# A two-layer spectral and MLP network on one core: weight table with the zero frequency kept in its rows, and a rewritten step order for the first layer

## The chip, the cores and the metric

The kernel runs on one core of one Trainium2 chip. A core has a matrix engine (PE, with its weight loads listed apart as PEld), three elementwise engines (DVE, ACT, POOL), a queue engine that mostly starts transfers (SP), and DMA engines that all queues share. The metric is device time in microseconds (us); lower is better. The time before is the median of six runs.

## The reference

The input `x` has 2048 rows of 512 bf16 values. Two layers are applied, each made of a spectral filter and an MLP mixer, with the same weights in both:

```python
def _A_ref(x, w_r, w_i):
    B, S, D = x.shape
    X = jnp.fft.rfft2(x.astype(jnp.float32), axes=(-2, -1))
    X = X * (w_r + 1j * w_i)
    return jnp.fft.irfft2(X, s=(S, D), axes=(-2, -1)).astype(jnp.bfloat16)

def _B_ref(x, w1, w2, w3, w4):
    h = _gelu(_layernorm(x) @ w1)          # 512 -> 512
    hs = shifted_quarters(h) @ w2          # each quarter of h moved by -1, +1, -2, +2 rows
    x1 = x + hs
    return x1 + _gelu(_layernorm(x1) @ w3) @ w4   # 512 -> 1792 -> 512

for _ in range(2):
    x = x + _A_ref(_layernorm(x), A_w_r, A_w_i)
    x = x + _B_ref(_layernorm(x), B_w1, B_w2, B_w3, B_w4)
```

The filter weights `A_w_r` and `A_w_i` are 2048 x 257: one value for each of 2048 sequence frequencies and 257 feature frequencies, of which number 0 is the constant term. The layer norm takes the mean away, so that the constant term of every row is zero and the kernel works with the 256 frequencies 1 to 256 only.

## The kernel before

**Layout.** Row s = 16p + q of `x` lies in partition p, slot q, of `x_state`. The two-dimensional transform is split into three products with small tables: over p, over d (the feature index) and over q. The frequencies are then held in 32 index pairs j, two of which make one of 16 blocks b.

**Start.** `load_all` (L152) issues all loads on SP's queue: eight pieces of `x`, table FA, half of table TL, and then the filter weights in four chunks of eight j (`for lo in range(0, NH, 8)`, L174), each chunk for the real plane (pl 0) and the imaginary one (pl 1), with two halves of table TR and the rest of TL in between; at the end come G and Tinv. `load_W` (L200) fills partitions 0 to 31 of the tile `W` from rows 64m + j (L205), and partitions 32 to 63 from rows 64m + 64 - j, in falling order (L206; the row for j = 0 apart, L208). Partitions 64 to 127 are a copy of 0 to 63, made by a transfer within SBUF that POOL issues (L209); these eight copies are put off with `K.later` until the first front has been issued. `W` is 128 x 2 x 32 x 256 bf16, and each j of a plane takes 256 neighbouring values. `load_mlp` (L185) issues on SP a tiny transfer that reads the last chunk's copy in `W`, and behind it the four MLP weight matrices.

**First front.** `first_front` (L391) does layer norm statistics and the product over p for the first layer (`over_p`, results moved to tile V). `wake` and `fill` (L219, L230) run matmuls on a tile of zeros to keep PE busy.

**A layer.** `layer` (L441) runs a hand-written list of steps, `ORDER_A` for the first layer and `ORDER_B` for the second. Each token is a letter (the step), a number (which block, unit or row), a PSUM bank after a dot, or A or V for ACT or DVE. The schedule is manual: instructions enter each engine's queue in the order of the list and every engine works through its queue in order. A unit is one block (0, 1, 14, 15) or two (2, 4, 6, 8, 10, 12). The steps of the spectral part are:

- `d` (L455): product over d of a unit on PE, L462; `t` moves it to SBUF (tile TV) on ACT or DVE.
- `q` (L476): product over q on PE, L486; `x` moves it to tile X.
- `p` (`weigh`, L493): two DVE products of X with `W`, one for each plane, into tile PB (L501). This is the step that needs the filter weights.
- `N` (`negate`): negates a half of TR on DVE (L698), needed by `b`.
- `b` (L504): back over q on PE, L510; `m` moves it to tile M.
- `D` (L523): back over d on PE, L528. It contracts over the frequencies for one slot of M, which holds part of every block, so that the first `D` waits for the last `m`.
- `Y`, `P`, `a`: move, back over p (L540), and add to `x_state` (L548).

Then come norm, transposes, and the MLP: `v` and `h` (first matrix, L579, and gelu), `u` and `f` (second matrix, L595), `w` and `g` (third, L630), `W` and `A` (fourth, L643, and the sum). During the first layer's MLP sixteen steps `L` (`permute`, L687) reorder the frequencies inside `W` for the second layer: one DVE copy out to a tile X (L692) and one back (L693). At the end of the first layer, `O` and `G` do the second layer's product over p.

Of the kernel before, what the change touches and what calls it, by code (L numbers as in the profile page):

```python
# [13 lines left out]
BF16 = dt.bfloat16  # L14
FP32 = dt.float32

P = 128
# [5 lines left out]
NH = 32  # L23
# [75 lines left out]
def kernel(  # L99
# [24 lines left out]
    K.bank, K.next_bank = None, 0  # L124
    ctx.enter_context(tc.manual_schedule())
    load_all(K, A_x, A_w_r, A_w_i, B_w1, B_w2, B_w3, B_w4)
    make_hT(K)
    wake(K)
    first_front(K)
    for last in (False, True):  # L130
# [21 lines left out]
def load_all(K, A_x, A_w_r, A_w_i, B_w1, B_w2, B_w3, B_w4):  # L152
    nc = K.nc
    tabs = dft_tables()
    dram = {k: nc.inline_tensor(v, name="tab_" + k).ap() for k, v in tabs.items()}

    def table(k, eng):
        t = K.const.tile(list(tabs[k].shape), BF16, name=k)
        eng.dma_start(t[:], dram[k])
        setattr(K, k, t)  # L160

    K.x = K.big.tile([P, NQ, D], BF16, name="x_state")
    xv = A_x[0].rearrange("(p q) d -> p q d", q=NQ)
    table("T", nc.scalar)
    for h in range(8):
        nc.sync.dma_start(K.x[:, h * 2:h * 2 + 2, :], xv[:, h * 2:h * 2 + 2, :])  # L166
    table("FA", nc.sync)
    K.TL = K.const.tile(list(tabs["TL"].shape), BF16, name="TL")
    K.TR = K.const.tile([P, 3, NH, 64], BF16, name="TR")
    load_q = lambda k, sl: nc.sync.dma_start(getattr(K, k)[:, sl], dram[k][:, sl])  # L170
    load_q("TL", slice(0, 8))
    K.W = K.const.tile([P, 2, NH, 256], BF16, name="W")
    K.later = []
    for lo in range(0, NH, 8):  # L174
        for pl, w in enumerate((A_w_r, A_w_i)):
            load_W(K, w, pl, lo, lo + 8)
        if lo == 8:
            load_q("TL", slice(8, 16))
        if lo in (0, 16):
            nc.sync.dma_start(K.TR[:, 0:2, lo:lo + 16], dram["TR"][:, :, lo:lo + 16])  # L180
    for k in ("G", "Tinv"):
        table(k, nc.sync)
    K.load_G2 = lambda: nc.sync.dma_start(K.G[:], dram["G2"])

    def load_mlp():  # L185
        gate2 = K.const.tile([1, 16], BF16, name="gate2")
        nc.sync.dma_start(gate2[:], K.W[64:65, 1, NH - 1, 0:16])
        for k, w, n, c in (("w1", B_w1, 4, D), ("w2", B_w2, 4, D), ("w3", B_w3, 4, FH), ("w4", B_w4, 14, D)):
            t = K.const.tile([P, n, c], BF16, name=k)
            nc.sync.dma_start(t[:], w.rearrange("(t p) n -> p t n", p=P))  # L190
            setattr(K, k, t)

    K.load_mlp = load_mlp
    K.eps = K.const.tile([P, 1], FP32, name="eps")
    nc.vector.memset(K.eps[:], EPS)
    K.mhalf = K.const.tile([P, 4], FP32, name="mhalf")
    nc.gpsimd.memset(K.mhalf[:], -0.5)


def load_W(K, w, pl, lo, hi):  # L200


    v = w.rearrange("(m j) f -> m j f", j=64)[:, :, 1:257]
    j1 = max(lo, 1)
    K.nc.sync.dma_start(K.W[0:32, pl, lo:hi], v[:, lo:hi])  # L205
    K.nc.sync.dma_start(K.W[32:64, pl, j1:hi], v[:, 65 - hi:65 - j1][:, ::-1])  # L206
    if lo == 0:
        K.nc.sync.dma_start(K.W[32:64, pl, 0], v[:, 32])  # L208
    K.later.append(lambda: K.nc.gpsimd.dma_start(K.W[64:128, pl, lo:hi], K.W[0:64, pl, lo:hi]))  # L209


# [7 lines left out]
def wake(K):  # L219

    nc = K.nc
    t = K.const.tile([P, 256], BF16, name="zeros")
    nc.vector.memset(t[:], 0.0)
    one = K.small.tile([P, 1], FP32, name="wake")
    nc.scalar.activation(one[:], K.eps[:], ACT.Sqrt, bias=0.0, scale=1.0)
    K.zeros = t
    fill(K, WAKE)


def fill(K, n):  # L230
    for i in range(n):
        K.nc.tensor.matmul(K.ps[:, 7 if K.bank is None else K.bank, 0:256], lhsT=K.zeros[:, 0:P], rhs=K.zeros[:], start=True, stop=True)


class Stats:
# [155 lines left out]
def first_front(K):  # L391
# [26 lines left out]
    def front(k):  # L418
        ps[k] = over_p(K, FIRST[k])
        if k in FILL:  # L420
            fill(K, FILL[k])
# [19 lines left out]
def layer(K, last):  # L441
# [3 lines left out]
    nc = K.nc  # L445
# [47 lines left out]
    def weigh(u):  # L493
        n = len(UNITS[u])
        x = X.pop(u)[:, :, 0:256 * n].rearrange("p h (n f) -> p h n f", f=256)
        pab[u] = []
        for pl in range(2):
            t = PB[:, n_pab[0] % 8]
            n_pab[0] += 1
            w = K.W[:, pl, 2 * u:2 * u + 2 * n].rearrange("p (n h) f -> p h n f", h=2)  # L500
            nc.vector.tensor_tensor(t[:, :, 0:n], x, w, op=ALU.mult)  # L501
            pab[u].append(t)

# [182 lines left out]

    def permute(k):  # L687

        w = K.W[:, k // 8, 4 * (k % 8):4 * (k % 8) + 4]
        t = K.stream.tile([P, 4, 256], BF16, name="X", bufs=2)  # L690
        tw = t[:]
        nc.vector.tensor_copy(tw.rearrange("p b (h f) -> p b h f", h=2), w.rearrange("p b (f h) -> p b h f", h=2))  # L692
        nc.vector.tensor_copy(w, tw)  # L693

    def negate(k):
# [3 lines left out]

    next_V = {}  # L700
    table = {"d": over_d, "t": take_d, "q": over_q, "x": take_q, "p": weigh, "b": back_q,
             "D": back_d, "Y": take_D, "P": back_p, "a": add_x, "s": stats2, "r": rstd2, "c": lambda g: ln[g].ratio(), "n": norm2,
             "T": tr, "v": w1, "h": gelu1, "u": w2, "f": add_x1, "k": square3, "E": resid,
             "R": rstd3, "o": norm3, "U": tr3, "w": w3, "g": gelu3,
             "m": take_b, "W": w4, "A": add_x2, "y": store, "B": stats4, "j": aggr4, "S": rstd4, "Q": scale_T,
             "O": front, "G": take_front, "L": permute, "N": negate}
    for op in (ORDER_B if last else ORDER_A).split():
        op, _, bank = op.partition(".")
        K.bank = int(bank) if bank else None
        if op[0] == "X":  # L710
            fill(K, int(op[1:]))
            continue
        if op[0] in FLEX:
            table[op[0]](int(op[1:-1]), op[-1])
        else:
            table[op[0]](int(op[1:]))
# [16 lines left out]
Q15V O3 Q14V G4A O5 G3V O7 G5A O8 G8A G7V  # L733
"""
ORDER_A = """
d4.0 d1.2 d2.4 t1A q1.2 t2A t4V x1V q4.0 d10.6 q2.4 x4A p1 t10V d6.2 d12.0 q10.6 x2A t6A p4 N0 d8.4 q6.2 t12A t8A
b1.0 x10V d15.1 p2 b4.6 b3.7 m1A x6A b5.0 m4A t15V d14.1 q8.2 m3A b2.6 p10 d0.7 m5A N1 p6 q12.4 b10.0 t14V x8A
q15.2 x12A t0A p8 m2A x15A b11.1 m11A p12 q0.4 b6.7 b8.6 m6A p15 x0A q14.2 x14V b7.1 m10A b9.7 m7A m9A b13.4 p0
b15.5 b12.0 p14 m15A m15V m12A b0.1 b14.7 m8V m13V m0A m14A D2.4 D3.6 Y3A D0.0 Y2V P4.4 a4 Y0A P7.5 P6.6 P5.7 D1.0
a7 a6 a5 D4.4 s4 P0.6 Y1V s7 P1.7 s6 a0 s5 P3.0 Y4A r1 a1 P2.1 s0 a3 P8.6 P9.7 a2 D5.4 a8 D7.0 n7V n6V n5V T3 s1  # L740
n4V s3 s2 T2 r0 a9 D6.2 Y5A P11.6 Y7A s8 P10.4 P15.5 Y6A P13.7 a11 a10 s11 n2V n3V a15 n0V P14.6 n1A a13 c1 s10
P12.4 s9 r2 a12 s15 L7 a14 v3.2 n10V s12 n9V s13 s14 T1 v2.4 h3 n8A T0 n11V L12 r3 h2 n12V v1.6 h1 v0.2 T5 h0 c0
n15V n14A u3.6 T4 u2.7 u1.2 v5.4 f1 n13V u0.3 L15 h5 v4.0 f2 T7 T6 f3 E2 f0 u4.2 E3 v6.6 h4 k1 f4 L6 L1 v7.2 k3
u5.0 E4 c3 u6.1 k0 f5 E0 u7.4 k2 c2 R0 h7 h6 E1 o0V f6 k4 o1V o2A u10.5 u9.0 f7 u8.1 o3V u14.4 u12.6 f10 k5 f8
u11.1 U0 L9 k6 k7 f9 u13.5 R1 E5 u15.0 f12 E7 f14 f13 U1 E9 E8 w4.6 o4A E6 f11 L5 o5V o6V o7A w0.4 k10 k8 k9 w5.2
g0 E13 w1.4 f15 E14 k12 U3 E11 k11 k13 U2 g4 E12 k14 w2.0 E10 w6.6 R2 g5 w7.2 g1 o9V g7 o11V g6 k15 w3.4 g2 o10A R3
g3 o8A L0 w13.2 w9.6 w12.0 L3 w11.4 o14A E15 U4 g13 g12 L10 o13V U5 g11 W1.0 g9 W2.1 W3.6 L11 o15A w10.4 w8.2 L4
g10 o12V L2 L13 A1 g8 L8 A3 A2 W0.4 w14.2 A0 B2 W5.5 B0 L14 B3 g14 U6 W7.4 A5 B1 A7 B7 w20.2 w19.4 j1 j2 W6.0 j0 j7
g19 W4.1 U7 A6 g20 w15.2 w24.4 w21.6 B5 A4 g21 g15 w16.0 B6 j3 B4 w17.6 w23.2 g16 j6 w27.0 j5 g17 g27 w18.6 j4 g18
S0 w25.0 Q0 W9.6 Q3 S1 W10.7 g25 A10 g24 Q2 B10 w22.4 W8.7 Q1 g23 A9 Q4 O1.2 g22 Q7 w26.4 Q6 B9 W11.6 O0.0 G1A j9  # L750
Q5 g26 G1V A8 B8 O2.4 G0A A11 B11 G2A j11 W14.7 W12.6 j10 G2V A14 B14 j14 j8 G0V A12 S14 Q14 B12 W15.7 j12 A15 B15
j15 W13.6 O14.7 S2 S12 Q9 Q11 O3.0 Q12 S15 Q8 Q10 O4.4 G14A G3A Q15 A13 B13 G4A j13 G3V S13 O5.6 X4.2 O15.2 Q13 G4V
G15V G5A G15A X4.3 O6.6 G6A X8.3
"""
ORDER_B = """
d15.0 t15A d4.2 q15.0 x15V d1.4 t4A d8.6 t1A q1.4 q4.2 p15 t8A x1V b15.0 d12.6 x4A p1 m15V m15A q8.4 t12A d10.0
# [45 lines left out]
```

## Time and profile before

| What | us |
|---|---|
| Median of 6 runs | 365.51 |
| Lowest and highest of them | 363.57, 367.26 |
| The profiled execution's own time | 365.26 |
| Its span, first to last instruction | 363.3 |
| PE busy in the span | 344.1 |
| ACT busy | 199.2 |
| DVE busy | 183.5 |
| First layer: first `d` product to first `D` product (L462 at 22.38, L528 at 49.36) | 26.98 |
| Second layer: the same (L462 at 199.08, L528 at 219.74) | 20.66 |
| The eight copies L209, issue to landing (least, median, greatest) | 4.0, 8.2, 8.8 |

Start times are counted from the span's start. Busy time on PE includes the matmuls on zeros. The time of a run is about 2 us longer than the span, so that a change in the span is a change in the time.

### The profile page before, as it was taken

What the parts mean: (1) busy time and instruction counts of PE and PEld (TensorE: products, weight loads), DVE (VectorE), ACT (ScalarE), POOL (GpSimd) and SP (SyncE); (2) the same over time, 40 slices, a digit from 0 to 9 for tenths busy, and PEclk for the clock granted to TensorE, in tenths of its full rate; (3) what the DMA queues carried; (4) which work ended last, traced back from release to release, by engine and by line L of the source; (5) the groups of instructions that cost most, each with busy time, mean ns of one, the idle gap of its engine ahead of it and who ended that gap; (6) DMA issues with size and microseconds to landing.
All of it is one profiled execution on the core that took longest, in us unless ns stands there. A gap on an engine that the chain in (4) does not pass through costs nothing.

```text
span 363.3 us, 5613 instructions
## 1 busy us (share of the span) xinstructions
PE 344.1 (95%) x2124; PEld 188.9 (52%) x2124; DVE 183.5 (50%) x453; ACT 199.2 (55%) x343; POOL 67.0 (18%) x171
## 2 busy tenths in 40 slices
PE   7798698899999999999998999999999999999996
PEld 5676487434444444444546788734444444444442
DVE  3866679758965342402677797846680031100122
ACT  6868669968579122054304997987785510247100
POOL 1211006752331000200031000781450000000000
PEclk9899899999999999999999999999999999999999
DMA  7999594540234200000000000452322032000012
GB/s 240 241 229 219 153 362 99 97 87 14 47 58 88 58 0 2 0 0 2 1 2 0 2 2 0 78 109 51 58 52 38 0 58 74 0 29 2 29 43 87
DMA packets 47274, 24.60 MB, mean 68 GB/s; under 512 B 34832, under 2 KB 44048, under 8 KB 47248
## 3 DMA queue, kind: packets, MB, share of 16 engines
q1 hardware_dynamic: 46464, 22.09, 26.2%
q0 software_dynamic: 640, 2.10, 2.6%
q8 instruction: 16, 0.26, 0.3%
q14 instruction: 10, 0.08, 0.1%
q10 hardware_dynamic: 144, 0.07, 0.1%
HBM read 11.67 MB, written 2.10 MB: 38 GB/s over the span
## 4 chain that ended last, share of the span: by engine, by line
PE 73%; DMA 10%; ACT 9%; DVE 3%; issue 2%; SPq 1%; POOL 0%; ACTq 0%; DVEq 0%; POOLq 0%
PE ps L630 27%; PE ps L643 26%; PE ps L595 8%; PE ps L579 5%; ACT junk L258 4%; DMA W<-in_A_w_i_dram 3%; PE ps L510 2%; DMA W<-W 2%; DMA TL<-tab_TL 2%; PE ps L462 2%; PE ps L486 2%; DMA W<-in_A_w_r_dram 2%; PE ps L528 2%; ACT Y L149 1%; SPq L166 1%
## 5 line engine op out<-in xcount | busy, mean ns | idle before, releaser
L637 ACT ACTIVATE gT<-ps 128x1024 bf16<-128x1024 f32 x56 | 54.9, 1023 | 86.5 <-PE ps L630 86.5
L643 PE MATMUL ps<-w,gT 128*128 128x512 bf16 x448 | 98.8, 379 | 0.0
L630 PE MATMUL ps<-xT,w 128*128 128x512 bf16 x448 | 98.6, 379 | 0.0
L648 DVE TENSOR_TENSOR x_state<-ps,x_state 128x512 bf16<-128x512 f32 x32 | 21.7, 689 | 121.1 <-PE ps L643 121.0
L630 PEld LDWEIGHTS <-w 128*128 128x128 bf16 x448 | 43.8, 98 | 52.6
L643 PEld LDWEIGHTS <-gT 128*128 128x128 bf16 x448 | 43.8, 98 | 52.6
L579 PE MATMUL ps<-xT,w 128*128 128x512 bf16 x128 | 29.2, 379 | 1.4 <-ACT hT L586 0.9
L603 DVE SCALAR_TENSOR_TENSOR xn<-xn,ln_c,ps 128x512 bf16<-128x512 bf16 x32 | 23.1, 744 | 13.2 <-PE ps L595 8.9
L595 PE MATMUL ps<-w,hT 128*128 128x512 bf16 x128 | 29.0, 379 | 0.8 <-ACT hT L586 0.8
L501 DVE TENSOR_TENSOR PB<-X,W 128x1024 bf16<-128x1024 bf16 (+1 forms) x40 | 21.3, 579 | 5.2 <-DMA W<-W 1.7
L258 ACT ACTIVATE junk<-x_state 128x512 bf16<-128x512 bf16 x36 | 22.6, 629 | 1.1
L548 DVE SCALAR_TENSOR_TENSOR x_state<-ps,x_state 128x512 bf16<-128x512 f32 x32 | 20.5, 686 | 3.5 <-PE ps L540 3.5
L258 ACT ACTIVATE junk<-xn 128x512 bf16<-128x512 bf16 x32 | 20.1, 627 | 3.6 <-DVE xn L603 3.1
L586 ACT ACTIVATE hT<-ps 128x512 bf16<-128x512 f32 x32 | 17.5, 607 | 7.9 <-PE ps L579 7.9
L246 DVE BATCH_NORM_STATS2 ln_st<-x_state 128x6 f32<-128x512 bf16 x28 | 18.7, 685 | 4.9 <-DMA x_state<-in_A_x_dram 4.7
L579 PEld LDWEIGHTS <-w 128*128 128x128 bf16 x128 | 12.3, 98 | 16.6 <-issue 1.5
L595 PEld LDWEIGHTS <-hT 128*128 128x128 bf16 x128 | 12.4, 98 | 16.4 <-ACT hT L586 1.2
L510 PE MATMUL ps<-TR,PB 128*128 128x128 bf16 x256 | 18.1, 225 | 3.0 <-DVE TR L698 1.8
L510 PEld LDWEIGHTS <-PB 128*128 128x128 bf16 x256 | 15.5, 101 | 6.6 <-issue 4.6
L149 ACT ACTIVATE V<-ps 128x1024 bf16<-128x1024 f32 (+2 forms) x11 | 9.5, 884 | 15.8 <-PE ps L351 14.1
L281 POOL TENSOR_SCALAR ln_ve<-ln_mv 128x4 f32<-128x4 f32 (+1 forms) x15 | 3.9, 261 | 76.9 <-DVE ln_mv L274 76.2
L462 PE MATMUL ps<-FA,V 128*128 128x256 bf16 x128 | 16.3, 273 | 1.7 <-ACT V L149 1.7
(73 smaller groups left out, 388.7 us busy)
## 6 DMA issues: line engine op xcount, KB each, us to landing
w<-in_B_w_dram SPq DMA_DIRECT2D x2, 1792.0 KB, 13.5
x_state<-in_A_x_dram SPq DMA_DIRECT2D x8, 256.0 KB, 5.6
W<-W POOLq DMA_DIRECT2D x8, 256.0 KB, 8.2
out_dram<-x_state SPq DMA_DIRECT2D x16, 128.0 KB, 1.8
TR<-tab_TR SPq DMA_DIRECT2D x2, 512.0 KB, 9.2
w<-in_B_w_dram SPq DMA_DIRECT2D x2, 512.0 KB, 4.2
W<-in_A_w_r_dram SPq DMA_DIRECT2D x7, 128.0 KB, 8.5
W<-in_A_w_i_dram SPq DMA_DIRECT2D x7, 128.0 KB, 9.5
```

The costliest lines, as they stand in the source:

```text
L258: K.nc.scalar.activation(junk[:], src, ACT.Square, bias=0.0, scale=D ** -0.5, accum_out=self.s[:, i, 1:2])
L462: nc.tensor.matmul(oi[:, 1 - h], rhs=K.FA[:, t, h], lhsT=V[:, 2 * t + h, 2 * b:2 * b + 2].rearrange("d b q c -> d (b q c)"), start=(t == 0 ...
L501: nc.vector.tensor_tensor(t[:, :, 0:n], x, w, op=ALU.mult)
L510: nc.tensor.matmul(o[:, (2 * h + F) * P:(2 * h + F + 1) * P], lhsT=pab[u][k][:, h, b - u, F * P:(F + 1) * P], rhs=K.TR[:, k:k + 2, 2 * b + ...
L548: nc.vector.scalar_tensor_tensor(K.x[:, q, :], ps.pop(("P", q)), 1.0, K.x[:, q, :], op0=ALU.mult, op1=ALU.add, accum_out=ln[g].s[:, i, 0:1])
L579: nc.tensor.matmul(o[:, i], lhsT=K.w1[:, t, j * P:(j + 1) * P], rhs=xT[g][:, :, t, :], start=(t == 0), stop=(t == 3))
L595: nc.tensor.matmul(o, lhsT=K.hT[:, j, st:st + P], rhs=K.w2[:, j, :], start=(j == 0), stop=(j == 3))
L603: nc.vector.scalar_tensor_tensor(xn[:, q, :], xn[:, q, :], ln[q // 4].c[:, q % 4:q % 4 + 1], ps.pop(("u", n)), op0=ALU.mult, op1=ALU.add, ...
L630: nc.tensor.matmul(o[:, i], lhsT=K.w3[:, c, t * P:(t + 1) * P], rhs=xT3[g][:, :, c, :], start=(c == 0), stop=(c == 3))
L637: nc.scalar.activation(gT[g][:, 2 * j:2 * j + 2, :], ps.pop(("w", k)), ACT.Gelu_apprx_tanh, bias=0.0, scale=1.0)
L643: nc.tensor.matmul(o, lhsT=gT[g][:, t, i * P:(i + 1) * P], rhs=K.w4[:, t, :], start=(t == 0), stop=(t == 13))
L648: nc.vector.tensor_tensor(K.x[:, q, :], ps.pop(("W", n)), K.x[:, q, :], op=ALU.add)
```

## The change

`W` is widened to 257 values for each j. The weights' view `v` in `load_W` keeps all 257 columns. The load of partitions 0 to 31 now takes eight whole rows of 257, which lie one behind the other both in DRAM and in the tile. The loads of partitions 32 to 63 still take columns 1 to 256 of each row, now into positions 1 to 256 of the tile's rows. Position 0 in partitions 32 to 63 is set to zero on POOL at the start, since the copy to partitions 64 to 127 reads whole rows. `weigh` and `permute` read and write positions 1 to 256, so that the rows they use begin at an odd element of the tile, 514 bytes apart.

The tile of zeros is cut from 256 to 128 columns, and `fill` reads it twice for one matmul.

`ORDER_A` is replaced by another list of the same 475 steps: other order, other banks, and another choice of ACT or DVE for 26 of the moves and norms. `ORDER_B` and `ORDER_0` are the same.

```diff
-    K.W = K.const.tile([P, 2, NH, 256], BF16, name="W")
+    K.W = K.const.tile([P, 2, NH, 257], BF16, name="W")
     K.later = []
+    nc.gpsimd.memset(K.W[32:64, :, :, 0:1], 0.0)
...
-    v = w.rearrange("(m j) f -> m j f", j=64)[:, :, 1:257]
+    v = w.rearrange("(m j) f -> m j f", j=64)
     j1 = max(lo, 1)
     K.nc.sync.dma_start(K.W[0:32, pl, lo:hi], v[:, lo:hi])
-    K.nc.sync.dma_start(K.W[32:64, pl, j1:hi], v[:, 65 - hi:65 - j1][:, ::-1])
+    K.nc.sync.dma_start(K.W[32:64, pl, j1:hi, 1:257], v[:, 65 - hi:65 - j1, 1:257][:, ::-1])
     if lo == 0:
-        K.nc.sync.dma_start(K.W[32:64, pl, 0], v[:, 32])
+        K.nc.sync.dma_start(K.W[32:64, pl, 0, 1:257], v[:, 32, 1:257])
     K.later.append(lambda: K.nc.gpsimd.dma_start(K.W[64:128, pl, lo:hi], K.W[0:64, pl, lo:hi]))
...
-    t = K.const.tile([P, 256], BF16, name="zeros")
+    t = K.const.tile([P, P], BF16, name="zeros")
...
-        K.nc.tensor.matmul(K.ps[:, 7 if K.bank is None else K.bank, 0:256], lhsT=K.zeros[:, 0:P], rhs=K.zeros[:], start=True, stop=True)
+        K.nc.tensor.matmul(K.ps[:, 7 if K.bank is None else K.bank, 0:256], lhsT=K.zeros[:], rhs=K.zeros[:].unsqueeze(1).to_broadcast([P, 2, P]), start=True, stop=True)
...
-            w = K.W[:, pl, 2 * u:2 * u + 2 * n].rearrange("p (n h) f -> p h n f", h=2)
+            w = K.W[:, pl, 2 * u:2 * u + 2 * n, 1:257].rearrange("p (n h) f -> p h n f", h=2)
...
-        w = K.W[:, k // 8, 4 * (k % 8):4 * (k % 8) + 4]
+        w = K.W[:, k // 8, 4 * (k % 8):4 * (k % 8) + 4, 1:257]
...
 ORDER_A = """
-d4.0 d1.2 d2.4 t1A q1.2 t2A t4V x1V q4.0 d10.6 q2.4 x4A p1 t10V d6.2 d12.0 q10.6 x2A t6A p4 N0 d8.4 q6.2 t12A t8A
-b1.0 x10V d15.1 p2 b4.6 b3.7 m1A x6A b5.0 m4A t15V d14.1 q8.2 m3A b2.6 p10 d0.7 m5A N1 p6 q12.4 b10.0 t14V x8A
-q15.2 x12A t0A p8 m2A x15A b11.1 m11A p12 q0.4 b6.7 b8.6 m6A p15 x0A q14.2 x14V b7.1 m10A b9.7 m7A m9A b13.4 p0
-b15.5 b12.0 p14 m15A m15V m12A b0.1 b14.7 m8V m13V m0A m14A D2.4 D3.6 Y3A D0.0 Y2V P4.4 a4 Y0A P7.5 P6.6 P5.7 D1.0
...
+d1.0 d0.1 d4.2 t1A t0V q0.0 x0V q1.4 d6.6 x1V t4A p0 d2.0 t6A q4.4 d10.2 t2V q6.6 x4A p1 N0 p4 d8.4 t10A t8V x6A p6
+q2.0 b1.2 b4.3 m1A d12.6 b0.2 m4A d14.3 x2A q10.4 t12A p2 d15.0 b5.1 t14V x10A m0V q8.6 b2.3 b6.4 x8A m2A m6A m5A
+q12.6 q14.2 N1 p10 b7.5 t15A p8 b10.4 m7V b11.1 b3.0 x12A m11A x14V p12 p14 m3A b8.5 m8A q15.6 m10A b9.2 x15A p15
+b12.3 b13.5 m12A m9A b14.4 m13V b15.3 m15V m14A m15A D0.2 D1.4 Y1A Y0V D3.6 P1.2 P0.3 P2.4 a1 P3.5 Y3A a0 a2 a3
...
```

## The prediction

> **What bounds the kernel now.** I read the page first, for where PE has gaps; then a table of busy times by stage; then the waits and the order of time of DVE in the stage that stood out.
>
> ```profile
> span 363.3 us, 5613 instructions
> PE   7798698899999999999998999999999999999996
> ```
>
> PE is full from about 80 us on, apart from a dent near 195. What can be won lies in the first eight slices of 9.1 us. Stages, from the table of windows (columns: busy us and count for PE, PEld, DVE, ACT, POOL, then clock, DMA share, GB/s):
>
> ```profile
> 22.30:30.00 7.70, 7.62 (x78) 5.82 (x79) 4.66 (x6) 5.87 (x7) 1.03 (x3) 1.00 1.09 229
> 30.00:38.00 8.00, 6.63 (x81) 4.47 (x79) 4.81 (x8) 4.87 (x7) 1.02 (x2) 1.00 0.98 197
> 38.00:49.40 11.40, 7.82 (x100) 6.40 (x101) 9.54 (x19) 8.73 (x15) 0.00 (x0) 0.85 0.68 229
> 49.40:69.20 19.80, 18.74 (x149) 14.37 (x150) 16.33 (x46) 17.42 (x40) 9.25 (x27) 1.00 0.63 169
> 94.80:189.60 94.80, 94.80 (x458) 43.71 (x457) 43.16 (x106) 37.48 (x52) 11.07 (x22) 1.00 0.10 20
> 199.10:219.80 20.70, 19.84 (x257) 15.36 (x258) 16.89 (x30) 18.45 (x27) 0.00 (x0) 1.00 0.01 2
> ```
>
> The first three rows are the first layer's stage from the first `d` to the first `D`: 27.1 us, PE busy 22.1. The last row is the same stage of the second layer, with the weights long in place: 20.7 us. So at most 27.0 - 20.7 = 6.3 us are to be had there; the MLP row (94.8 of 94.8) has nothing to give. DVE in the first of these stages, waits and then single products:
>
> ```profile
> DVE PB L501 <- DMA W<-W: 1.7, 1, 1.7
> DVE X L147 <- PE ps L486: 1.7, 2, 1.3
> DVE TV L147 <- PE ps L462: 1.5, 1, 1.5
> DVE PB L501 <- DMA W<-in_A_w_r_dram: 1.4, 1, 1.4
> ...
> 28.57 0.69 DVE L501 TENSOR_TENSOR PB<-X,W 128x1024 bf16<-128x1024 bf16 x1 [0.67 <-DMA TR<-tab_TR]
> 30.62 0.69 DVE L501 TENSOR_TENSOR PB<-X,W 128x1024 bf16<-128x1024 bf16 x1 [1.36 <-DMA W<-in_A_w_r_dram]
> 35.46 0.69 DVE L501 TENSOR_TENSOR PB<-X,W 128x1024 bf16<-128x1024 bf16 x1 [0.84 <-DVE TV L147]
> 37.89 0.69 DVE L501 TENSOR_TENSOR PB<-X,W 128x1024 bf16<-128x1024 bf16 x1 [1.74 <-DMA W<-W]
> ```
>
> By the list, the products are `p1`, then `p4` (28.57 and 30.62, weights of chunk 8), `p2`, then `p10` (35.46 and 37.89, chunk 16). Up to 38 DVE is busy 9.5 of 15.7 us; then it runs without rest (9.54 of 11.4), as six units still wait behind `p10`: `p6 p8 p12 p15 p0 p14`. Two of them (6 and 0) use chunks 8 and 0, which had long landed. The chain of waits shows the same:
>
> ```profile
> 29.41 8.46 DMA W<-W
> 37.87 0.02 issue
> 37.89 0.70 DVE PB L501
> ```
>
> The copy of chunk 16's second plane, issued at 29.41, ends the wait. The last two copies are issued at 34.02 and 36.39 (timeline of POOL), and SP's tiny transfer behind the last one is issued at 40.39 (timeline of SP): chunk 24 is there by 40.4.
>
> **What the Trainium skill says.** (1) "VectorE: DVE Perf Modes", section on Mode 2×_1P, asks of two bf16 values a clock that the data be 4-byte aligned. (2) "Vector Engine (DVE) Microarchitecture Reference", section 5.1, reports from measurements that 4-byte alignment makes no difference. After the change every other row of `W` starts 2 bytes off. The trace of before has only aligned rows: the 1024-element product takes 687 ns and the 512-element one 420, so 512 more elements cost 267 ns, 1.9 a nanosecond; it can't say which page holds. (3) "DMA: Bandwidth & Descriptors", Specifications, wants at least 512 bytes a transfer for full rate. The rows of 256 values are just that. The trace fits a penalty for such small pieces: 329 GB/s between 5 and 11 us, when mostly `x` in pieces of 2 KB moves, against 229 between 22.4 and 30, when the weights' 512-byte pieces and copies share the engines.
>
> **The change part by part.**
>
> *Order.* The new list takes the units as `p0 p1 p4 p6 p2 p10 p8 p12 p14 p15`. Behind `p10` stand four units instead of six, and all four need chunk 16 or 24. Durations from the rows by shape in this stage: a pair of products 1.28 us (unit of two blocks) or 0.76 (one block); a TV move on DVE 1.30 or 0.73, an X move 0.69, an M move 0.68, half of one 0.42, a negation 0.42. DVE's work in the new list: six pairs 7.7, four 3.0, `t2 t8` 2.6, `t0 t14` 1.5, `x0 x1 x14` 2.1, `m0 m7 m13` 2.0, half of `m15` 0.4, `N0 N1` 0.8: 20.1 us, as good as the old list's 20.0. ACT comes to 18 us (4 double and 2 single `t`, 6 double and 1 single `x`, 12.5 `m` at 0.5 to 1.0). With the arrivals of before left as they are:
>
> - DVE starts at 23.4 (first `d`, about 1 us of PE after 22.4): `t0 x0 x1 p0` until 26.8, `t2 p1 N0` until 29.3.
> - `p4`: its second product waits for 30.6 as before; done 31.3. `t8 p6 p2` need nothing late: 35.1. `t14 m0 N1`: 36.9.
> - `p10`: second product at 37.9, done 38.6. This wait shrinks from 1.7 to about 0.3. `p8` 39.9, `m7 x14` 41.2.
> - `p12`, with chunk 24 there at 40.4: 42.5. `p14 p15`: 44.0. Then `b15`, `m13`, both halves of `m15`: the first `D` at 45.4.
>
> ACT's `x` for each `p` comes out before its use in the same count (`x10` 35.3 for 36.9, `x12` 39.3 for 41.2, `x15` 42.0 for 43.3). So 49.4 becomes 45.4. I give back 0.4 for hand-overs I counted too short and for PE at half speed in part of 38 to 49 (mean clock 0.85): first `D` at 45.8, gain 3.6. The least that I allow is 2.0.
>
> *The rest of the list.* From `D` to the first L630 the first layer takes 45.4 us (49.4 to 94.8) and the second 43.2 (219.8 to 263.0): two lists of the same kinds of steps, 2.2 us apart, bounded by ACT and PE by turns. The new tail after the last fourth-matrix product has one `O` less (O4 O5 O15 O6 O14 against O14 O3 O4 O5 O15 O6), but ends on it. I take 0, and +-1.5 for the range.
>
> *Loads.* Half of the weights, 1.05 MB, goes in pieces of 4112 bytes instead of 512. At 229 GB/s these are 4.6 us of transfers, at 329 3.2: 1.4 us gained at most on chunk 24, less on the others. Against it, the other half is written to positions 2 bytes off. The trace has no such write: from no cost to, say, half as much again (+2.3 us). I take the two as even: 0, with chunk 24 between 39.0 and 42.7. By the count above, `p12` has 0.8 us of slack, so +2.3 costs 1.5 and -1.4 gains at most the waits left at `p4` and `p10`, 0.9. The copies grow from 4096 to 4112 bytes a row and plane: nothing.
>
> *POOL, zeros, permute.* The memset has 32 x 64 values; memsets of 128 x 64 take 0.38 and 0.57 us. POOL is then idle from 1.4 to 7.0, and SP comes to the first load of partitions 32 to 63 at 7.3: hidden. `fill` streams 256 columns as before. If the copy back in `permute` (0.43 us) loses a mode it costs up to 0.26 us sixteen times, 4.2 us of DVE, beside an MLP stage with 43 of 95 us busy: hidden.
>
> *Sum.* -3.6 from the order, 0 for the rest. Against the profiled execution's own 365.26 (span 363.3): 361.7. The median of the runs is 0.25 higher, so I say 361.8.
>
> **Rivals.**
>
> *Given back later.* The gain at `D` is eaten by the new list further on (a worse tail at 190 to 200 or the ACT-bound stretch 49 to 69): 365. For: the two lists' 2.2 us between `D` and L630. Against: PE is full from 95 to 190 and passes a gain on.
>
> *The weights' unaligned rows halve DVE's rate in `weigh`* (the slower side). Place: L501 in both layers. Price: the move of 1024 elements that takes one a clock (X, fp32 from PSUM) is 1.22 us against 0.69, so 12 x 0.53 + 8 x 0.27 = 8.5 us of DVE a layer. DVE then needs 28.6 us in the first layer (first `D` at 54, +4.5) and 25.4 in the second, where it begins at 201.0 (+5): 374.8. It decides from about 3.6 us of DVE loss a stage. For: page (1). Against: page (2), which measured.
>
> *The unaligned 512-byte writes are slow.* If they take three times as long (+9.2 us, -1.4 for the whole rows), chunk 24 lands at 48.2; then `p12 p14 p15` and the last `b` and `m` need 4.6: `D` at 52.8, +3.4: 368.7. It turns slower only from a chunk 24 later than 44.8, 4.4 us late.
>
> *All weights in time:* if the loads gain their full 1.4 us and the new list does as well as the second layer's, `D` comes at 43.1: 359.0.
>
> **How the numbers follow.** Forecast 0.57, given back 0.16, DVE rate 0.09, slow writes 0.12, all in time 0.06. About 0.5%, 1.8 us, can be told from no change. Faster: nine tenths of the forecast, all of the last, a fifth of the slow writes: 0.60. Same: the rest of the forecast, most of the second case, some of the writes: 0.22. Slower: 0.18. The likeliest case alone reaches from 359.5 to 364.0; the range goes on to the slow writes, 368.7, and leaves out the DVE rate above and little below: 359.0 to 369.0.
>
> **What would show it.** First L528 at 45 to 46.5, against 49.4; in DVE's timeline no wait over 0.7 us before `p10`, and `p12` after `p8`. Mean of L501 unchanged at 579 ns; near 1000 would prove the DVE rival. SP's tiny transfer issued at 39 to 42; after 45 it is slow writes. From D to the first L630 44 to 47 us; more means given back. I am wrong if the first `D` comes early and the time does not follow, or if it does not come early.

## The result, and the profile after

The changed kernel takes 362.51 us in the median of 33 runs (359.6 to 367.15). The kernel before, run beside it, takes 366.04 (68 runs). The ratio is 0.9909, with a 95% interval of 0.9893 to 0.9925: 0.9% faster, a little over 3 us. The medians are of all runs, while a ratio leaves out the slow runs, those over 1.5% above the fastest run of their kernel.

The page of the changed kernel's profiled execution, which took 364.63 us, 2.1 over its own median:

```profile
span 362.5 us, 5619 instructions
PE   7896988899999999999999999989999999999996
```

Its stages, from the table of windows (columns as before). The first three rows are the first layer's stage from the first `d` to the first `D`, the last is the second layer's:

```profile
22.00:30.00 8.00, 7.62 (x76) 5.62 (x78) 5.07 (x9) 5.63 (x6) 1.53 (x3) 1.00 1.08 232
30.00:38.00 8.00, 5.32 (x52) 3.69 (x48) 5.08 (x7) 4.18 (x5) 1.02 (x2) 0.80 1.03 198
38.00:48.80 10.80, 9.21 (x137) 7.34 (x134) 9.10 (x17) 9.33 (x16) 0.51 (x1) 0.99 0.64 200
...
94.10:189.00 94.90, 94.90 (x465) 44.07 (x464) 45.17 (x113) 36.89 (x48) 9.35 (x20) 1.00 0.10 20
198.00:218.70 20.70, 19.83 (x258) 15.34 (x258) 16.93 (x30) 18.45 (x27) 0.00 (x0) 1.00 0.01 2
```

The MLP stretch and the second layer's stage are what they were (94.9 and 20.7 us). The first layer's stage still has gaps: DVE is busy 10.2 us of the 16 up to 38, and PE has only 5.32 busy in the second row. The first `D` comes at 48.79 us, against 49.36. That is 0.6 us, not the 3 that the runs show. DVE's waits in this stage, and its products in order of time, say why (in the changed file the product stands on L502):

```profile
DVE PB L502 <- ACT X L149: 1.7, 3, 1.0
...
DVE PB L502 <- DMA W<-W: 1.5, 1, 1.5
DVE PB L502 <- DMA W<-in_A_w_r_dram: 0.9, 1, 0.9
...
30.90 0.69 DVE L502 TENSOR_TENSOR PB<-X,W 128x1024 bf16<-128x1024 bf16 x1 [1.05 <-ACT X L149]
33.11 0.69 DVE L502 TENSOR_TENSOR PB<-X,W 128x1024 bf16<-128x1024 bf16 x1 [1.52 <-DMA W<-W]
34.92 1.28 DVE L502 TENSOR_TENSOR PB<-X,W 128x1024 bf16<-128x1024 bf16 x2
39.86 2.50 DVE L502 TENSOR_TENSOR PB<-X,W 128x1024 bf16<-128x1024 bf16 x4
```

In this execution the weights came later than in the trace of before. The second product of `p4` starts at 33.11, not at 30.62, and the copies of chunk 24 are issued at 36.09 and 38.36, against 34.02 and 36.39. Behind `p4` no product waits for weights any more: `p10` and `p8` go through as four products on end from 39.86. The two traces are therefore not at the same point of their spread, and the experiments below bring a second trace of each kernel.

One number makes all traces comparable. From the first `D` to the end of the span there are 363.3 - 49.36 = 313.9 us before and 362.5 - 48.79 = 313.7 after. A run is 2.0 to 2.1 us longer than its span. If this rest is as steady in the runs without a profile, the medians 366.04 and 362.51 stand for a first `D` at about 50.1 and 46.7 us (an estimate from these figures): all but some 0.2 us of the gain is made before `D`.

### The profile page after: what moved, and what is told of

Read it like the earlier page. It is cut to its first block, busy times and chain, and to the rows that moved or that the text cites. A ratio compares the mean times of both kernels' runs of the same rounds, so it can differ in the third digit from the quotient of the medians.

```text
span 362.5 us, 5619 instructions
## 1 busy us (share of the span) xinstructions
PE 343.9 (95%) x2124; PEld 188.9 (52%) x2124; DVE 183.5 (51%) x453; ACT 199.9 (55%) x343; POOL 66.5 (18%) x172
## 4 chain that ended last, share of the span: by engine, by line
PE 76%; DMA 9%; ACT 9%; DVE 2%; issue 2%; SPq 0%; ACTq 0%; DVEq 0%; POOLq 0%
PE ps L644 27%; PE ps L631 27%; PE ps L596 7%; PE ps L580 5%; ACT junk L259 4%; PE ps L463 3%; DMA W<-W 3%; PE ps L511 3%; DMA W<-in_A_w_r_dram 2%; DMA W<-in_A_w_i_dram 2%; PE ps L487 2%; ACT Y L149 2%; PE ps L529 2%; DMA x_state<-in_A_x_dram 1%; ACT M L149 1%
## 5 line engine op out<-in xcount | busy, mean ns | idle before, releaser
L502 DVE TENSOR_TENSOR PB<-X,W 128x1024 bf16<-128x1024 bf16 (+1 forms) x40 | 21.3, 581 | 5.0 <-ACT X L149 1.7
L259 ACT ACTIVATE junk<-xn 128x512 bf16<-128x512 bf16 x32 | 20.1, 627 | 6.0 <-DVE xn L604 5.5
L463 PE MATMUL ps<-FA,V 128*128 128x256 bf16 x128 | 17.1, 281 | 1.1 <-ACT V L149 0.7
L529 PE MATMUL ps<-G,M 128*128 128x256 bf16 x128 | 15.3, 273 | 1.9 <-ACT M L149 1.9
```

The lines of the kernel that those rows point to most:

```text
L259: K.nc.scalar.activation(junk[:], src, ACT.Square, bias=0.0, scale=D ** -0.5, accum_out=self.s[:, i, 1:2])
L463: nc.tensor.matmul(oi[:, 1 - h], rhs=K.FA[:, t, h], lhsT=V[:, 2 * t + h, 2 * b:2 * b + 2].rearrange("d b q c -> d (b q c)"), start=(t == 0 ...
L529: nc.tensor.matmul(o[:, i, e * 256:(e + 1) * 256], lhsT=M[:, F, e, 2 * m + i, :], rhs=K.G[:, F, e, :], start=(F == 0), stop=(F == 1))
```

## The experiments

Theory A: the new order makes the gain, as it leaves fewer steps behind the weights that land last; the wide rows and whole-row reads cancel each other. Theory B: the whole-row reads bring the weights earlier. A third: the new list is simply better, late weights or not. All runs, with marks from one trace each ("behind last copy" is the issue of SP's tiny transfer that waits for the last copy). Each ratio is to runs of the kernel before on the same chip; e1 to e4, e5 to e8 and e9 to e12 ran on three different chips, with 5 to 22 runs of each:

| Kernel | Ratio to before, 95% interval | Behind last copy, us | First d, us | First D, us | Span, us |
|---|---|---|---|---|---|
| before | | 40.39 | 22.38 | 49.36 | 363.3 |
| changed | 0.9909, 0.9893 to 0.9925 | 41.66 | 22.01 | 48.79 | 362.5 |
| e1 order only | 0.9877, 0.9848 to 0.9906 | 42.11 | 21.81 | 48.08 | 362.0 |
| e2 loads only | 1.0043, 1.0017 to 1.0068 | 43.21 | 23.41 | 54.06 | 368.0 |
| e3 no whole rows | 0.9974, 0.9947 to 1.0000 | 45.33 | 21.63 | 51.05 | 364.8 |
| e4 changed again | 0.9888, 0.9858 to 0.9918 | 42.28 | 23.44 | 48.07 | 361.8 |
| e5 early weights, new order | 0.9842, 0.9801 to 0.9882 | 41.98 | 24.24 | 46.12 | 359.4 |
| e6 early weights, old order | 0.9782, 0.9753 to 0.9812 | 41.87 | 23.49 | 44.92 | 358.9 |
| e7 changed, tables later | 0.9945, 0.9900 to 0.9990 | 43.05 | 22.18 | 49.28 | 363.3 |
| e8 order only, tables later | 0.9903, 0.9867 to 0.9939 | 41.07 | 22.88 | 46.41 | 360.7 |
| e9 order only, two tables | 0.9832, 0.9795 to 0.9869 | 40.85 | 23.44 | 46.25 | 360.2 |
| e10 changed, two tables | 0.9852, 0.9809 to 0.9895 | 40.11 | 21.41 | 46.76 | 360.5 |
| e11 before, two tables | 0.9968, 0.9944 to 0.9993 | 40.42 | 22.96 | 49.74 | 363.8 |
| e12 before again | 0.9989, 0.9962 to 1.0017 | 43.60 | 24.41 | 53.12 | 367.1 |

From the first `D` to the end every trace has 313.3 to 314.3 us, while the first `D` itself moves from 44.9 to 54.1. Nothing in the rest of the list gives or takes more than this 1 us. One trace each is a small sample: the two traces of the kernel before (first row and e12) have their last copies 3.2 us apart.

**e1, the order alone.**

```diff
 (before.py)
 ORDER_A = """
-d4.0 d1.2 d2.4 t1A q1.2 t2A t4V x1V q4.0 d10.6 q2.4 x4A p1 t10V d6.2 d12.0 q10.6 x2A t6A p4 N0 d8.4 q6.2 t12A t8A
...
+d1.0 d0.1 d4.2 t1A t0V q0.0 x0V q1.4 d6.6 x1V t4A p0 d2.0 t6A q4.4 d10.2 t2V q6.6 x4A p1 N0 p4 d8.4 t10A t8V x6A p6
...
```

> Before with the new order of the first layer alone; W, its loads and the tile of zeros as before. Theory A (the order does it all, because fewer steps are left behind the late weights): ratio to before 0.990 (0.987 to 0.994), about 362.5 us. Theory B (the whole-row reads bring the weights earlier and that is the gain): 1.000 (0.997 to 1.003). Theory C (both, half each): 0.995.

0.9877: all of the gain, with the loads of before. So the new list makes it, and theory B has nothing left to explain. What in the list makes it is the question of e4, e12, e5 and e6.

**e2, all but the order.**

```diff
 (changed kernel, with ORDER_A of before)
 ORDER_A = """
-d1.0 d0.1 d4.2 t1A t0V q0.0 x0V q1.4 d6.6 x1V t4A p0 d2.0 t6A q4.4 d10.2 t2V q6.6 x4A p1 N0 p4 d8.4 t10A t8V x6A p6
...
+d4.0 d1.2 d2.4 t1A q1.2 t2A t4V x1V q4.0 d10.6 q2.4 x4A p1 t10V d6.2 d12.0 q10.6 x2A t6A p4 N0 d8.4 q6.2 t12A t8A
...
```

> The changed kernel with the old order of the first layer put back; the wide W, the whole-row reads and the cut tile of zeros stay. Theory A: ratio to before 1.000 (0.997 to 1.004), nothing gained by the loads, and the first D product at 49 to 50 us as before. Theory B: 0.991. If the rows that begin 2 bytes off make the other half of the reads slow: above 1.004, and the first D after 50 us.

1.0043, and the interval excludes 1: the new loads bring nothing and cost a little with this order. This is the third of the cases expected (above 1.004, first `D` after 50 us); the first `D` of its trace is the latest of all, 54.06.

**e3, wide rows without whole-row reads.**

```diff
-    nc.gpsimd.memset(K.W[32:64, :, :, 0:1], 0.0)
+    nc.gpsimd.memset(K.W[0:64, :, :, 0:1], 0.0)
...
-    K.nc.sync.dma_start(K.W[0:32, pl, lo:hi], v[:, lo:hi])
+    K.nc.sync.dma_start(K.W[0:32, pl, lo:hi, 1:257], v[:, lo:hi, 1:257])
```

> The changed kernel with both halves of the weights read as columns 1 to 256 into positions 1 to 256, so no read takes whole rows and all of them are written 2 bytes off. Theory A: ratio to before 0.990 to 0.993, within 0.3% of the changed kernel. If whole rows pay for the rows that begin 2 bytes off: 0.995 or more, since then twice as many reads have that cost.

0.9974, against 0.9888 for the changed kernel on the same chip: the intervals do not touch. SP's transfer behind the last copy, from the timeline of SP in e1 (rows of 256), then e3 (all rows written as pieces of 512 bytes, 514 bytes apart), then the changed kernel again, e4 (half of them whole rows):

```profile
42.11 0.61 SPq L187 DMA_DIRECT2D gate<-W  x1
```

```profile
45.33 0.61 SPq L188 DMA_DIRECT2D gate<-W  x1
```

```profile
42.28 0.61 SPq L188 DMA_DIRECT2D gate<-W  x1
```

With the order held fixed, such pieces for all rows cost about 1% of the time (0.9974 against 0.9877, intervals apart), and whole rows for half of them take most of it back. The last weights are 3.2 us later in e3's trace than in e1's. That size is not firm: e3's mark is the latest of the nine traces with this order of loads, but the other eight spread over 3.2 us themselves, from 40.4 to 43.6. So the two edits of the loads nearly cancel. A small cost seems to be left: the wide version is behind the narrow one in all four pairs of one order and one order of loads (e2 by 0.4% behind before, e4 by 0.1% behind e1, e7 by 0.4% behind e8, e10 by 0.2% behind e9), though only e2's difference is clear of the noise.

**e4 and e12, both kernels once more.** No edit.

> The changed kernel itself, on the same chip as the three beside it and as a second sample of its trace: ratio 0.991 (0.988 to 0.994). The first D product, at 48.8 us in the trace already seen, comes at 45 to 47.5 us if that trace had its weights unusually late (its time was 2 us over the median), at 48.5 to 49 if the gain is made after D.

> The kernel before once more, for a second sample of its trace: ratio 1.000 (0.997 to 1.003). If the trace of before already seen had its weights early (last copy issued at 36.4, against 38 to 38.7 in all others), the first D comes at 50 to 52 us here instead of 49.4, and the rest from D to the end is again 313.7 to 314.0 us.

The ratios repeat (0.9888; 0.9989). Neither first `D` lies where it was expected: 48.07 us is between the two cases for e4, and 53.12 is later than the 50 to 52 for e12. The timeline of DVE, e12 first, then e4:

```profile
33.04 0.69 DVE L501 TENSOR_TENSOR PB<-X,W 128x1024 bf16<-128x1024 bf16 x1 [1.13 <-DMA W<-in_A_w_r_dram]
...
36.32 0.74 DVE L147 CAST TV<-ps 128x512 bf16<-128x512 f32 x1
41.14 0.69 DVE L501 TENSOR_TENSOR PB<-X,W 128x1024 bf16<-128x1024 bf16 x1 [4.08 <-issue]
42.08 0.69 DVE L501 TENSOR_TENSOR PB<-X,W 128x1024 bf16<-128x1024 bf16 x1 [0.25 <-DMA W<-W]
...
44.84 3.28 DVE L501 TENSOR_TENSOR PB<-X,W 128x1024 bf16<-128x1024 bf16 x6
```

```profile
33.41 0.69 DVE L502 TENSOR_TENSOR PB<-X,W 128x1024 bf16<-128x1024 bf16 x1 [1.29 <-DMA W<-in_A_w_r_dram]
...
39.16 0.69 DVE L502 TENSOR_TENSOR PB<-X,W 128x1024 bf16<-128x1024 bf16 x1
40.63 1.90 DVE L502 TENSOR_TENSOR PB<-X,W 128x1024 bf16<-128x1024 bf16 x3 [0.78 <-DVE PB L502]
```

In both, `p4`'s second product comes at 33.0 to 33.4. In the old order only `N0 x10 p2 t15` follow, and then DVE stands 4.1 us before `p10`. The view names no releaser ("issue"), but its X had been moved at 33.98, and the first copy of chunk 16 had been issued at 32.80 only: I read the wait as one for that copy. In the new order the time goes to `t8 p6 p2 t14 m0 N1`, and `p10` starts at 39.16 without a wait, its second product after 0.8 us. Chunk 16's first copy is 3.6 us earlier in e4 (29.23), so the two waits are not to be compared by themselves. What comes after them is: from `p10`'s second product to the first `D` the old order needs 11.0 us here and 11.5 in its first trace (37.89 to 49.36), the new one 7.4 (40.63 to 48.07). In the four traces of the old order with late weights it is 11.0 to 12.0 us (e2 and e11 too), in the eight of the new one 7.4 to 8.4. That is what is left behind late weights. The whole stage is 28.7 us in e12 and 24.6 in e4.

Not all of the difference is DVE's own work. In the four traces of the old order DVE also waits 0.9 to 1.3 us there for a product over q, before the move `x14`. In the first trace (timeline of DVE, then windows with columns as before):

```profile
45.27 0.69 DVE L147 CAST X<-ps 128x512 bf16<-128x512 f32 x1 [1.34 <-PE ps L486]
```

```profile
42.00:45.00 3.00, 2.75 (x24) 1.88 (x23) 1.90 (x4) 2.76 (x7) 0.00 (x0) 0.50 0.86 283
```

The wait runs from 43.9 to 45.3 us, and for most of it PE worked at a granted clock of 0.50. The new order has no such wait before `x14`.

**e5 and e6, no weight late.**

```diff
-            w = K.W[:, pl, 2 * u:2 * u + 2 * n, 1:257].rearrange("p (n h) f -> p h n f", h=2)
+            w = K.W[:, pl, 2 * u % 8:2 * u % 8 + 2 * n, 1:257].rearrange("p (n h) f -> p h n f", h=2)
```

(and the same in the kernel before, without `1:257`). Every product takes its weights from the first chunk, so these two kernels leave out three quarters of the weights; all loads and copies still run.

> The changed kernel in which every unit of weigh takes its weights from the first chunk (rows 2u modulo 8), so that no product waits for a late chunk; all loads and copies still run. It computes with the wrong weights for three quarters of the frequencies. Theory A (the new order is there for the late weights, DVE's work is the floor): first D product at 44.5 to 46 us, ratio to before 0.982 to 0.987. If the floor lies elsewhere: no better than the changed kernel, 0.990.

> The kernel before with the same edit of weigh, wrong weights for three quarters of the frequencies as above. Theory A: with nothing late the two orders are alike, first D at 44 to 46, ratio 0.981 to 0.988, within 0.3% of e5. Rival (the new order is simply the better list, late weights or not): 0.3% or more behind e5, ratio above 0.988.

With no late weights the old order is as good as the new one or better: 0.9782 against 0.9842, intervals that just overlap. They were expected within 0.3% of each other and lie 0.6% apart, with the old order ahead. The two kernels differ in the row layout too, which may make part of that. In the traces the stage is 21.4 us for the old and 21.9 for the new. So the third theory falls: the new list isn't better where nothing is late. It pays for being less hurt by lateness. No run moved only `p6` and `p0` ahead of `p10` in the old list, so that the share of that step alone, beside the other moves of the new list, is not shown. The waits of DVE in e5 show the floor: no line with W is left, and DVE waits for PE and ACT only:

```profile
DVE TV L147 <- PE ps L463: 1.5, 1, 1.5
...
DVE PB L502 <- ACT X L149: 0.7, 2, 0.5
DVE X L147 <- PE ps L487: 0.6, 1, 0.6
```

**e7 and e8, weights ahead of the tables.** To use what the order leaves, the weights' chunks were moved ahead of tables TR and TL (e7 in the changed kernel, e8 in the kernel before with the new order):

```diff
-        if lo == 8:
+        if lo == 16:
             load_q("TL", slice(8, 16))
-        if lo in (0, 16):
-            nc.sync.dma_start(K.TR[:, 0:2, lo:lo + 16], dram["TR"][:, :, lo:lo + 16])
+        if lo in (8, 24):
+            nc.sync.dma_start(K.TR[:, 0:2, lo - 8:lo + 8], dram["TR"][:, :, lo - 8:lo + 8])
```

> The changed kernel with its tables moved behind weights: first half of TR after chunk 8, second half of TL after chunk 16, second half of TR after chunk 24. If the stage is bounded by when the weights land: chunk 8's copy lands about 2 us earlier, first D 1 to 2.5 us earlier, ratio 0.984 to 0.988. If by DVE alone, or if the tables turn late instead: 0.990 or above.

> The kernel before with the new order and with the same move of the tables, so aligned rows of 256 and no whole rows. Same reasoning as for the one with wide rows: 0.983 to 0.988 if the landing of the weights is the bound; within 0.2% of e7 if wide rows and whole-row reads cancel, as the first runs said.

Both missed: 0.9945 and 0.9903, no better than without the move, and 0.4% apart where 0.2% was expected at most. The weights did come earlier (chunk 8's copies issued at 18.67 and 20.05 in e7, against 22.70 and 23.79 in e4), but the second half of TR was now late for the second negation, by 1.6 us in e8's trace and more in e7's. DVE's longest wait in e7:

```profile
DVE TR L699 <- DMA TR<-tab_TR: 3.4, 1, 3.4
```

**e9, e10, e11: only two tables moved.** The second half of TR stays ahead of chunk 24, which tries the cause just named:

```diff
-        if lo == 8:
+        if lo == 16:
             load_q("TL", slice(8, 16))
-        if lo in (0, 16):
-            nc.sync.dma_start(K.TR[:, 0:2, lo:lo + 16], dram["TR"][:, :, lo:lo + 16])
+        if lo in (8, 16):
+            r = lo // 16 * 16
+            nc.sync.dma_start(K.TR[:, 0:2, r:r + 16], dram["TR"][:, :, r:r + 16])
```

> The kernel before with the new order, and of the tables only two moved: first half of TR after chunk 8, second half of TL after chunk 16; the second half of TR stays ahead of chunk 24, where e7 and e8 had it too late for the second negation (waits of 3.4 and 1.6 us). If that wait was all that ate the earlier weights: no DVE wait over 1 us from the first product to p12, stage from the first d to the first D at 22 to 23 us, ratio 0.982 to 0.987. If not: 0.988 to 0.990 as with the order alone.

> The changed kernel with the same two tables moved. Same as e9 if wide rows with whole-row reads cost nothing on balance: ratio 0.982 to 0.987, within 0.3% of e9; 0.3% or more behind it if the rows that begin 2 bytes off still cost.

> The kernel before with the same two tables moved and its own order. The old order takes p10 (chunk 16) fourth. Theory A: it is still caught by chunk 16, but 1 to 2 us less: ratio 0.990 to 0.997. If the old order is the better one as soon as weights come a little earlier (as with no weight late at all): 0.985 or below, level with e9.

With the new order: 0.9832 on the narrow rows and 0.9852 on the wide ones, with no wait for TR before the second negation in either trace. On the wide rows the interval lies clear of e7's, so the late table was what e7 lost by. e9 has the lowest ratio here of the kernels that use all the weights, level with e5, which waits for none; its interval overlaps those of e10 and e1. Its stage is 22.8 us; the products up to `p2` run without a wait for weights, and the one wait of this kind left is 1.2 us inside `p10`, against the 1 us expected at most (timeline of DVE):

```profile
30.19 1.27 DVE L502 TENSOR_TENSOR PB<-X,W 128x1024 bf16<-128x1024 bf16 x2
32.58 1.28 DVE L502 TENSOR_TENSOR PB<-X,W 128x1024 bf16<-128x1024 bf16 x2
...
38.82 1.90 DVE L502 TENSOR_TENSOR PB<-X,W 128x1024 bf16<-128x1024 bf16 x3 [1.23 <-issue]
```

e10's trace still has one wait of 3.1 us for a copy, and 25.4 us for the stage; its median is level with e9's. e11, the old order with the same loads, reaches 0.9968: it still waits for chunk 16, 4.3 us in its trace. So the move of the tables brings 0.3% with the old order, and 0.4% with the new one (e1 to e9, e4 to e10). The order pays alone, and these runs don't show that the two gain more together than the sum of both.

## Why the prediction was right

The forecast was -3.6 us; the medians differ by 3.5, the ratio of 0.9909 makes it 3.3. The steps:

- **The order makes it (-3.6).** Right, and shown by e1 and e2; e1's ratio makes it 4.5 us, with an interval of 3.5 to 5.6. The reason given, fewer units behind `p10`, fits what e12 and e4 show: 11.0 us from `p10`'s second product to `D` against 7.4. One reading behind it was wrong: from 38 us on DVE of the kernel before does not run without rest. The wait of 1.34 us for PE shown at e12 lies in that stretch, and the old order loses by it too.
- **The arrivals "of before".** This term was mis-sized. I took `p4` at 30.6, chunk 16 at 37.9 and chunk 24 at 40.4 from one trace, and that trace had the earliest weights of the nine with this order of loads: the transfer behind the last copy is at 40.4 there and at 41.7 to 45.3 in the other eight. So the first `D` was put at 45.8, and the traces of the changed kernel have it at 48.8 and 48.1, outside the 45 to 46.5 that the prediction named as its sign. The difference was hurt less, as the kernel before is late with its weights too: its second trace has the first `D` at 53.1, not at 49.4. That both kernels are late by about the same was luck; nothing in the count provided for it. In the medians, by the remainder after `D`, the forecast was 49.4 to 45.8 and the result about 50.1 to 46.7.
- **The floor.** DVE's 20.1 us of work, 1 us before it and about 2 us of waits and end gave 23.0 us for the stage without the allowance. e5, with nothing late, takes 21.9.
- **The loads cancel (0).** Right within the noise for the new order (e1 0.9877, e4 0.9888), but the four pairs at e3 all lean to a small cost, 0.1 to 0.4%. The two parts of the term, the cost of the shifted pieces and the gain of whole rows, are not shown apart in microseconds; e3 only shows that both are there.
- **The rest of the list (0).** Right: 313.9 and 313.7 us from `D` to the end.
- **The DVE rival** is excluded. The rows used begin at elements 1, 258, 515 and so on, so that every other one is off a 4-byte boundary by 2 bytes, not each. By shape, the changed kernel's products over both layers:

```profile
L502 DVE TENSOR_TENSOR PB<-X,W 128x1024 bf16<-128x1024 bf16 x24 | 15.3, 688 | 3.5 <-DMA W<-W 1.5 <-ACT X L149 1.3 <-PE ps L511 0.7
...
L502 DVE TENSOR_TENSOR PB<-X,W 128x512 bf16<-128x512 bf16 x16 | 6.1, 421 | 1.5 <-DMA W<-in_A_w_r_dram 0.9 <-ACT X L149 0.5
```

688 and 421 ns, where the aligned rows of the kernel before take 685 and 420 over both layers; even half of the price that the rival put on a long product, 0.53 us, would show. The copy back in `permute` stays at 429 ns (427 before). Of the two pages of the Trainium skill, "Vector Engine (DVE) Microarchitecture Reference", section 5.1, is right here, and the 4-byte condition in "VectorE: DVE Perf Modes", section on Mode 2×_1P, does not show.

- **The slow-writes rival** named a cost that e3 supports, and put it far too high: +9.2 us for half of the rows, where the changed kernel's two traces have the mark behind the last copy at 41.7 and 42.3, inside the 40.4 to 43.6 of the narrow rows.

What stays open: why e5's ratio lies 0.6% (2.2 us) over e6's when their stages differ by 0.5 in the traces, what sets the spread of the weights' arrival between executions, and whether the new order also brings the first `d` forward, which lies between 21.4 and 24.4 us without a clear tie to the order.

## What to carry to other kernels

Where an engine works through a fixed queue, a late input costs what stands behind it, so put work that needs nothing late ahead of it, and judge the order at the lateness that the machine has: the list that was no worse with early inputs (e6) was the worse one with late ones. Take arrival times from several traces before counting on them to 1 us. When a load is moved ahead, look up the first user of what it displaces (e7's gain went to one late table), and test layout and order apart, since here the layout alone was a small loss (e2).

## What the runs showed that I had not expected

- Weights written to SBUF as pieces of 512 bytes at a pitch of 514 cost time against a pitch of 512: with the same order 1% of the whole (0.9877 to 0.9974). That it is the transfers that are slower rests on one trace of each, with the last weights at 45.33 against 42.11, the latest of the nine by 1.7 us.
- PE's clock is granted lower about when PE stands waiting for what is behind these weights. Over 24 to 50 us the mean clock is 0.87 to 0.93 in nine of the ten traces where PE's longest wait there is 1.3 to 3.0 us (e4 is the tenth, with 1.8 us and 1.00), and 1.00 in the four where it is 0.9 to 1.0 us (e5, e6, e8, e9). In e12 it falls just as the six units left run (windows of e12; the clock is the column before the DMA share):

```profile
36.00:44.00 8.00, 4.45 (x58) 3.23 (x59) 3.66 (x7) 3.52 (x5) 1.02 (x2) 1.00 0.68 150
44.00:53.10 9.10, 7.15 (x92) 5.90 (x92) 7.74 (x16) 7.68 (x14) 0.00 (x0) 0.81 0.83 288
```

So a wait may cost more than its own length, as the wait before `x14` in the old order suggests. This is seen together in the traces, not tried by itself.
